# Even tables loaded to column 196 and mirrored on ScalarE; the first spread of feature D/2 made by products with a row-picking matrix

## The chip, the cores and the metric

The kernel runs on one core of a Trainium2 chip. The metric is device time in microseconds (us) of one execution, the median of several; lower is better. The engines are called as in the profile: PE is TensorE (PEld its weight loads), DVE is VectorE, ACT is ScalarE, POOL is GpSimd, SP is SyncE, which only issues transfers. They run on their own instruction streams, each in order, and wait for one another by semaphores. Transfers are issued on the queues of SP, ACT and POOL and are moved by 16 shared DMA engines.

## The reference

A Fourier mixing block over (batch 8, sequence 3136, model dimension 256), of which the real part is kept, and then a gated convolution block:

```python
X = np.fft.fft(x, axis=1)
X = np.fft.fft(X, axis=2)
x = X.real.astype(np.float32)

h = np.maximum(x @ w_in, 0.0)                       # 256 -> 1024
for k in range(3):                                  # taps along the sequence, zero padded
    conv_out += conv_w[k][None, None, :] * hp[:, k:k + S, :]
gate = 1.0 / (1.0 + np.exp(-conv_out))
return (h * gate @ w_out).astype(np.float32)        # 1024 -> 256
```

Input and output are float32, the weights come as float64 and are narrowed on the chip.

## The kernel before

**What is computed, and in which form.** Along the sequence only half of the frequencies are needed, since the input is real: per batch two tables of 128 rows by NK = 1569 columns are made, called P and Q (`PQ[b]`, tiles pt and qt). P holds 128 features of the cosine sums, Q 127 of the sine sums. The 128th row of Q's tile is not a row of Q: it holds the odd columns of the sums of feature D/2 = 128, which has no partner. The transform along the features and the matrix w_in are multiplied into one matrix G of 2 x 1024 columns (`blocks`, `column`; `ge` is the part for feature D/2). The main loop then goes through 8 batches x 4 chunks of columns x 8 blocks of 128 of the 1024 channels, 256 steps in all. In each step `seed` writes feature D/2's part, spread over all 128 partitions (`eb`), times `ge` into the accumulator pa; `products` adds two products with G into pb and pa; `copies` and `combine` form both halves of the sequence with the ReLU; `first_tap`, `middle` (a transfer that adds, issued by POOL), `last_tap`, `sigmoid` and `gate` make the gated convolution; `mm2`, five steps later, multiplies with w_out and stores.

**Where the sums along the sequence come from.** x is folded first (`fold_ops`, VectorE, `folds(0)` and `folds(1)` for the two halves of batch 0), which leaves four residues q of 98 rows each, split by even and odd frequencies. The folded data are the stationary operand; cosine and sine tables are the moving one. `tabs[0]` is the even table, 98 (or 99) partitions x 2 (cosine, sine) x 4 (q) x HE = 393 columns; `tabs[1]` the odd one with four kinds of 196 columns, of which two are loaded and two are made by ScalarE (`mirror_tables`, L305 to L310). `mend_row` halves one row of each. `scaled` (L211 to L219) makes turned copies of the folded data on ScalarE, which the `odd` units multiply with the even table at every second column. For batch 0 the units are run before the loop: four for the odd frequencies (`odd_even`, `odd`, for sine and cosine), in four parts each, so that parts 0 and 1, which need only the first half of the folds and q of 0 and 1, come ahead of parts 2 and 3; then `feature` (the even columns of feature D/2, one output row at partitions 0, 32, 64, 96), then `even_even` and `even` for sine and for cosine. Each unit has products, a copy by ScalarE and a `fin` on VectorE (on POOL for `feature`), which writes its columns of qt, pt or er.

**The spread of feature D/2.** For batch 0 its sums are put together in a one-row tile er of 1569 columns: `row` (L461) transfers the whole last row of qt there on ScalarE's queue, the `fin` of `feature` overwrites the even columns on POOL, `flip` changes signs of every fourth column on ScalarE, `store` writes er to DRAM, and `spread` loads it back, broadcast to 128 partitions, for chunks 1 to 3. Chunk 0 doesn't go through DRAM: a product of er's first 386 columns with a row of ones (`one`) spreads it, and ScalarE copies the result to `eb[0, 0]` (L941 to L945).

**Order around it.** All engines follow the order in which the program is written. At the start SP issues the loads of the first weights, of x for batch 0, then the feature matrix `dm`, the odd table (`load_odd`, four transfers), the even table (`load_even`, two transfers with whole rows of 4 x 393 columns for 48 partitions each), and then the other weights; POOL issues the few rows that are left (`rest_odd`, `rest_even`). TensorE first runs products whose result is not used (L890 to L893), until the data are there. Tiles named h come from a pool of six, tiles named g from one of seven, po from one of four accumulators.

Of the kernel before, what the change touches and what calls it, by code (L numbers as in the profile page):

```python
# [37 lines left out]
def kernel(  # L38
# [214 lines left out]
    MR = NP // 2 // 16 * 16  # L253
    assert NP == 2 * MR + 2

    def load_even(eng):

        to = tabs[0].rearrange("p s q i -> p s (q i)")
        for i in range(2):
            eng.dma_start(out=to[i:2 * MR:2], in_=dft_seq[0:MR, 0:2, HQ * i:HQ * (i + 1)]  # L260
                          .rearrange("p s q i -> p s (q i)"))

    def rest_even(eng):

# [37 lines left out]
            row = tabs[0][96:NP, st, HQ - 1] if par == 0 else tabs[1][96:NP, st, 1]  # L302
            act(row, row, AF.Copy, scale=half[96:NP])

    def mirror_tables():  # L305

        for to, of, s in ((2, 1, -1.0), (3, 0, 1.0)):
            for i in range(2):
                act(tabs[1][0:KR, to, :, i:QO:2], tabs[1][0:KR, of, :, i:QO:2], AF.Copy,
                    scale=-s if i else s)  # L310

    class Unit:

# [30 lines left out]
    def units(b):  # L344
# [83 lines left out]
        def feature():  # L428

            mms = []  # L430
            for i in range(2):
                for j, qs in enumerate(((3, 1), (2, 0))):
                    for c in range(2):
                        n = HO // 2 + 1 - c
                        o = 32 * (2 * j + c)
                        mms.append(product((slice(o, o + 1), slice(0, n)),
                                           lambda k, q, c=c: ea[b][0:k, c, q:q + 1], 0, qs[i],
                                           slice(c, HE, 2), i == 0, i == 1))

            def copy(p):  # L440
                a_["e"] = [asp.tile([P, HO + 2], F32, name="as", tag="as") for _ in range(2)]
                for j in range(2):
                    for c in range(2):
                        n = HO // 2 + 1 - c
                        o = 32 * (2 * j + c)
                        nc.scalar.copy(out=a_["e"][c][0:1, j * n:(j + 1) * n], in_=p[o:o + 1, 0:n])

            def fin(p):
                t = er[b]
                nh = HO // 2  # L450
                for c in range(2):
                    n = nh + 1 - c
                    a, bb = a_["e"][c][0:1, 0:n], a_["e"][c][0:1, n:2 * n]
                    gt(t[:, 2 * c:Q4 + 1:4], a, bb, op=ALU.add)
                    gt(t[:, M - 2 * c:Q4:-4], a[:, 0:nh], bb[:, 0:nh], op=ALU.subtract)
            return Unit(b, mms, copy, fin, True)
# [3 lines left out]

        def row():  # L461
            er[b] = erp.tile([1, NK], F32, name="er", tag="er")
            nc.scalar.dma_start(out=er[b], in_=PQ[b][1][P - 1:P, :])

        def flip():

            act(er[b][:, 3:NK:4], er[b][:, 3:NK:4], AF.Copy, scale=-1.0)

        def store():
            nc.sync.dma_start(out=ed[b:b + 1, 0:NK], in_=er[b])  # L470

        return (begin, [odd_even(1), odd(1), even_even(1), even(1), feature(), odd_even(0), odd(0),
                        even_even(0), even(0)], row, flip, store)

    class Feature:

# [201 lines left out]
            for f in self.parts(c0, c1):  # L678
                f()

    one = gp.tile([1, P], F32, name="one", tag="g")
    nc.gpsimd.memset(one, 1.0)
    ident = gp.tile([3 * NF, 3 * NF], F32, name="ident", tag="g")
    make_identity(nc, ident)
    cw24 = gp.tile([3 * NF, 1, P], F32, name="cw24", tag="g")
# [44 lines left out]
    for f in load_ops(0, 1, nc.sync, None, True):  # L730
        f()

    act(first_use, low, AF.Sigmoid)
    w_cv.narrow(0, 1)
    w_in[0].narrow(0, 2)
# [7 lines left out]
    load_even(nc.sync)  # L743
    rest_odd(nc.gpsimd)
    rest_even(nc.gpsimd)
    for i in (1, 2, 3):
        w_in[i].load(nc.sync)
    wout = const.tile([P, NF, D], F32, name="wout")
# [138 lines left out]
        gs.pop(s)  # L887


    for pool, tag, n in ((psa, "pa", 1), (psa, "pa", 1), (psb, "pb", 7)):  # L890
        p = pool.tile([P, 512], F32, name=tag, tag=tag)
        for _ in range(n):
            mm(p, w4[0][:, 0, 0:P], win[0][:, 0].rearrange("p t n -> p (t n)"), True, True)  # L893

    begin, us, row, flip, store = units(0)
    begin()

    nc.gpsimd.memset(PQ[0][1][96:P, :], 0.0)
# [11 lines left out]
    w_out = Weight(wout, moe_w_out.rearrange("(c p) o -> p c o", p=P),  # L910
                   lambda sh: xp.tile(sh, I32, name="raw", tag="xh"))
    w_out.load(nc.sync)
    blocks(0)
    column(0)
    mend_row(1, half)
    mirror_tables()
    folds(1)
    mend_row(0, half)
    for f in load_ops(1, 0, nc.sync):
        f()  # L920
    for i in range(2):
# [2 lines left out]
    for j, u in enumerate(odds):  # L924
        for i in range(2, 4):
            u.part(i)
        u.copy()
        if j == 3:
            row()
        u.fin()  # L930

    for i, u in enumerate(us[j] for j in (4, 2, 3, 7, 8)):
        u.matmuls(0, 1)
        u.copy()
        u.fin()
# [12 lines left out]
    per = len(chunks) * NF  # L948
# [197 lines left out]
```

## Time and profile before

| what | value |
|---|---|
| median of 3 runs | 1171.97 us (1171.69 to 1172.16) |
| the profiled execution's own time | 1169.8 us |
| its span | 1168.0 us |
| granted TensorE clock, mean over the span | 0.995 |
| PE busy | 1141.3 us (98%) |
| DVE busy | 975.7 us (84%) |
| ACT busy | 942.2 us (81%) |
| POOL busy | 608.9 us (52%) |
| products with w_out (po <- wout, g), 3072 instructions | 706.8 us |

The profile is of one execution; the span goes from its first instruction to its last, and all times in it count from the start of the span. A line of a timeline has the start, the duration, the engine, the line of the kernel (L93 is the helper that records every product), the operation, the tile written <- the tiles read, the shape and the number of instructions merged into it; in brackets stand the engine's idle time ahead of it and what ended it. A fp32 product is two instructions in the trace. PEclk is the share of the full TensorE clock that was granted. A wait for several semaphores is put down to the one that came last by the profile; where the engine that is named had long been done, it was another, often a transfer.

### The profile page before, as it was taken

To read this page: it belongs to the slowest core of one execution; us is meant where nothing else is said; L and a number is where in the kernel's file an instruction comes from. 1 tells how busy PE (TensorE), PEld (TensorE's weight loads), DVE (VectorE), ACT (ScalarE), POOL (GpSimd) and SP (SyncE) were. 2 spreads that over 40 slices of the span, in tenths; PEclk is the share of its full clock that TensorE was granted. 3 is DMA by queue.
4 is the path that set the end of the run, shared out by engine and by line. 5 is a ranking of instruction groups with operands and counts; after the bars stand their busy time and mean duration, and the time that the engine had idled before them with its cause. 6 is when DMAs were issued, how large, how long until landed. Compare 5 with 4: busy or idle time off the path is not lost.

```text
span 1168.0 us, 15898 instructions
## 1 busy us (share of the span) xinstructions
PE 1141.3 (98%) x4820; PEld 891.2 (76%) x4820; DVE 975.7 (84%) x1448; ACT 942.2 (81%) x1939; POOL 608.9 (52%) x738
## 2 busy tenths in 40 slices
PE   5999999999999999999999999999999999999998
PEld 3666787778778777877777777777778777777777
DVE  8699989998888889898887888779787778788885
ACT  3498878888888879888888888888887888898885
POOL 7256545676466464646455464655344344444443
PEclk9899999999999999999999999999999999999999
DMA  9667886776667686757675766856665656666654
GB/s 245 162 113 161 173 150 148 168 162 154 133 144 169 136 183 130 171 112 177 144 165 127 150 133 136 183 123 122 133 124 101 124 122 143 131 129 128 125 117 105
DMA packets 106200, 168.15 MB, mean 144 GB/s; under 512 B 31275, under 2 KB 61241, under 8 KB 106115
## 3 DMA queue, kind: packets, MB, share of 16 engines
q0 software_dynamic: 42160, 115.87, 51.6%
q1 hardware_dynamic: 63208, 51.13, 15.7%
q8 instruction: 38, 0.62, 0.2%
q14 instruction: 47, 0.39, 0.1%
q10 hardware_dynamic: 747, 0.14, 0.1%
HBM read 38.40 MB, written 25.74 MB: 55 GB/s over the span
## 4 chain that ended last, share of the span: by engine, by line
PE 79%; ACT 5%; DVE 4%; issue 2%; DMA 0%; DVEq 0%; ACTq 0%
PE po L93 49%; PE pb L93 12%; PE pa L93 12%; PE pd L93 6%; DVE g L830 1%; ACT g L845 1%; ACT nb L807 1%; ACT os L878 1%; ACT pa L786 0%; ACT g L821 0%; DVE h L815 0%; DVE g L854 0%; DMA out_dram<-os 0%; DVE xh L157 0%; DVE xh L173 0%
## 5 line engine op out<-in xcount | busy, mean ns | idle before, releaser
L93 PE MATMUL po<-wout,g 128*128 128x256 f32 x3072 | 706.8, 380 | 5.2 <-DVE g L854 4.4
L93 PEld LDWEIGHTS po<-wout,g 128*128 128x128 f32 x3072 | 581.5, 190 | 149.8 <-issue 19.3
L825 POOL DMA_DIRECT2D g<-h x256 | 227.8, 890 | 466.5 <-ACT g L821 295.4
L845 ACT ACTIVATE g<-g,cw 128x385 f32<-128x385 f32 (+2 forms) x512 | 292.3, 625 | 66.1 <-DVE g L830 65.2
L853 POOL TENSOR_TENSOR g<-g,h 128x385 f32<-128x385 f32 (+1 forms) x256 | 299.3, 1169 | 45.4 <-ACT g L845 43.8
L807 ACT ACTIVATE nb<-pb 128x386 f32<-128x386 f32 (+3 forms) x512 | 227.2, 499 | 110.4 <-PE pb L93 109.7
L815 DVE CUSTOM_DVE_ANT_0 h<-pa,nb 128x386 f32<-128x386 f32 (+3 forms) x512 | 264.5, 557 | 29.1 <-POOL h L792 20.4
L830 DVE SCALAR_TENSOR_TENSOR g<-h,cw,g 128x770 f32<-128x770 f32 (+1 forms) x256 | 282.5, 1104 | 0.0
L821 ACT ACTIVATE g<-h,cw 128x770 f32<-128x770 f32 (+1 forms) x256 | 244.5, 955 | 0.0
L93 PE MATMUL pb<-qt,G 127*128 127x387 f32 (+2 forms) x512 | 215.6, 502 | 2.1 <-ACT nb L807 1.7
L93 PE MATMUL pa<-pt,G 128*128 128x387 f32 (+2 forms) x512 | 213.2, 497 | 0.5 <-ACT pa L786 0.5
L854 DVE TENSOR_TENSOR g<-g,h 128x385 f32<-128x385 f32 (+1 forms) x256 | 190.2, 743 | 24.6 <-ACT g L845 24.5
L786 ACT ACTIVATE pa<-eb,ge 128x387 f32<-128x387 f32 (+2 forms) x256 | 155.5, 608 | 1.5 <-DVE h L815 1.2
L93 PEld LDWEIGHTS pa<-pt,G 128*128 128x128 f32 x512 | 97.4, 191 | 75.0 <-issue 18.3
L132 POOL DMA_INDIRECT xh<-in_x_dram,idx x64 | 93.8, 1466 | 20.1 <-issue 11.3
L93 PEld LDWEIGHTS pb<-qt,G 127*128 127x128 f32 x512 | 91.3, 191 | 11.0 <-ACT nb L807 4.5
L93 PE MATMUL pd<-tab,w 98*128 98x197 f32 (+2 forms) x448 | 97.8, 318 | 0.2 <-DVE as L419 0.2
L93 PEld LDWEIGHTS pd<-tab,w 98*128 98x128 f32 (+1 forms) x448 | 82.0, 191 | 9.3 <-ACT pa L786 0.6
L878 ACT COPY os<-po 128x256 f32<-128x256 f32 x196 | 57.3, 394 | 6.6 <-PE po L93 6.6
L168 DVE TENSOR_TENSOR xh<-xh 98x1024 f32<-98x1024 f32 (+1 forms) x32 | 47.9, 1497 | 0.1
L157 DVE TENSOR_TENSOR xh<-xh 98x1020 f32<-98x1020 f32 (+1 forms) x32 | 46.9, 1469 | 0.4 <-DMA xh<-in_x_dram,idx 0.4
L392 DVE TENSOR_TENSOR as<-as,pd 128x196 f32<-128x196 f32 x14 | 5.0, 359 | 36.1 <-ACT as L388 36.1
(143 smaller groups left out, 456.9 us busy)
## 6 DMA issues: line engine op xcount, KB each, us to landing
g<-h POOLq DMA_DIRECT2D x192, 385.0 KB, 4.0
g<-h POOLq DMA_DIRECT2D x64, 416.0 KB, 4.2
out_dram<-os SPq DMA_DIRECT2D x96, 256.0 KB
xh<-in_x_dram SPq DMA_DIRECT2D x16, 784.0 KB
eb<-ed SPq DMA_DIRECT2D x16, 193.5 KB
raw<-in_moe_w_in_dram SPq DMA_DIRECT2D x4, 512.0 KB
raw<-in_moe_w_out_dram SPq DMA_DIRECT2D x1, 2048.0 KB
eb<-ed SPq DMA_DIRECT2D x8, 209.0 KB
```

Of the source, the lines that this page charges most:

```text
L93: nc.tensor.matmul(o, l, r, start=start, stop=stop, skip_group_check=True)
L132: nc.gpsimd.indirect_dma_start(out=xh[b, h][0:NP, 7 - m].rearrange("p q d -> p (q d)"), out_offset=None, in_=bass.AP(tensor=x.tensor, offs ...
L786: act(pa[s][:, 0:n], eb[b, c], AF.Copy, scale=ge[:, f:f + 1])
L807: act(nb[s][:, i, cols], p[:, cols], AF.Copy, scale=-1.0 if i else 1.0)
L815: nc.vector._custom_dve(TENSOR_ADD_SAT, out=to, in0=a[:, cols], in1=c[:, i, cols], s0=BIG, s1=0.0)
L821: act(gs[s], hs[s][:, 0:n], AF.Copy, scale=cw[:, 0, s[2]:s[2] + 1])
L825: nc.gpsimd.dma_start(out=gs[s], in_=hs[s][:, 1:1 + n], accum_op=ALU.add)
L830: stt(out=g, in0=h[:, k:k + n], scalar=cw[:, k, f:f + 1], in1=g, op0=ALU.mult, op1=ALU.add)
L845: act(gs[s][:, c], gs[s][:, c], AF.Sigmoid, scale=cw[:, 1, s[2]:s[2] + 1])
L853: gt(g[:, p], g[:, p], h[:, p], op=ALU.mult)
L854: vt(g[:, v], g[:, v], h[:, v], op=ALU.mult)
L878: nc.scalar.copy(out=osb[:, j % 2], in_=pt[:, j % 2])
```

## The change

1. **Even table.** `load_even` loads only columns 0 to 196 (HM = 197 columns) of each q, in four transfers instead of two. A new function, `mirror_even(q)`, makes columns 197 to 392 on ScalarE, as a reversed copy with a sign, two instructions for each q. The rows that POOL loads (`rest_even`) come whole, as before.
2. **Odd mirrors.** `mirror_tables` takes a half h; each call makes four copies of half the size. The first call comes ahead of `blocks(0)`, the second behind `mirror_even(0)`.
3. **Filler products.** `keep_on(n)` is the old loop body with the unused products; `keep_on(2)` is run once more behind `column(0)`.
4. **First spread.** A matrix `sel` of 128 x 384 takes the place of `one`: its first 128 columns are one in row 127 and zero elsewhere, the next 128 are their negative, and of the last 128 only row 0 is used, which is one. `odd_first` multiplies it with the odd columns of qt (two products over 128 rows), `even_first` the one-row sums of `feature` with the row of ones (four products), all into one po accumulator; ScalarE copies it to `eb[0, 0]` behind `even_even(1)`.
5. **Q's row.** `row` only allocates er. `flip`, now behind all units, transfers the odd columns of Q's last row to er on SP's queue and changes signs on POOL; `store` and `spread` follow it.
6. **Smaller moves.** The memset of qt's rows 96 to 127 goes from POOL (L898) to VectorE, ahead of its first instruction; the sums of `feature` lie in a tile of the pool h instead of two of the pool as.

```diff
+    HM = HO // 2 + 1
+
     def load_even(eng):
-        to = tabs[0].rearrange("p s q i -> p s (q i)")
-        for i in range(2):
-            eng.dma_start(out=to[i:2 * MR:2], in_=dft_seq[0:MR, 0:2, HQ * i:HQ * (i + 1)]
-                          .rearrange("p s q i -> p s (q i)"))
+        for s in range(2):
+            for i in range(2):
+                eng.dma_start(out=tabs[0][i:2 * MR:2, s, :, 0:HM], in_=bass.AP(
+                    tensor=dft_seq.tensor, offset=dft_seq.offset + (s * NQ + HQ * i) * HE,
+                    ap=[[4 * NQ * HE, MR], [HE, HQ], [1, HM]]))
+
+    def mirror_even(q):
+        for st, s in enumerate(((1.0, 1.0), (-1.0, 1.0), (-1.0, -1.0), (1.0, -1.0))[q]):
+            of = st if q % 2 else 1 - st
+            act(tabs[0][0:KR, st, q, HM:HE][:, ::-1], tabs[0][0:KR, of, q, 0:HE - HM], AF.Copy, scale=s)
...
-    def mirror_tables():
+    def mirror_tables(h):
+        k = KR if h else NP
         for to, of, s in ((2, 1, -1.0), (3, 0, 1.0)):
             for i in range(2):
-                act(tabs[1][0:KR, to, :, i:QO:2], tabs[1][0:KR, of, :, i:QO:2], AF.Copy,
-                    scale=-s if i else s)
+                act(tabs[1][0:k, to, h, i:QO:2], tabs[1][0:k, of, h, i:QO:2], AF.Copy, scale=-s if i else s)
...
         def row():
             er[b] = erp.tile([1, NK], F32, name="er", tag="er")
-            nc.scalar.dma_start(out=er[b], in_=PQ[b][1][P - 1:P, :])
+
+        def odd_first(p, n):
+            for i in range(2):
+                mm(p[:, 1 + 2 * i:n:4], sel[:, i * P:(i + 1) * P], PQ[b][1][:, 1 + 2 * i:n:4], i == 0, True)
+
+        def even_first(p, n):
+            for c in range(2):
+                m = (n - 2 * c + 3) // 4
+                o = HO // 2 + 1 - c
+                for i in range(2):
+                    mm(p[:, 2 * c:n:4], sel[0:1, 2 * P:3 * P], a_["e"][c][0:1, i * o:i * o + m], False, i == 1)
 
         def flip():
-            act(er[b][:, 3:NK:4], er[b][:, 3:NK:4], AF.Copy, scale=-1.0)
+            nc.sync.dma_start(out=er[b][:, 1:NK:2], in_=PQ[b][1][P - 1:P, 1:NK:2])
+            nc.gpsimd.tensor_scalar(out=er[b][:, 3:NK:4], in0=er[b][:, 3:NK:4], scalar1=-1.0, scalar2=None, op0=ALU.mult)
...
-    one = gp.tile([1, P], F32, name="one", tag="g")
-    nc.gpsimd.memset(one, 1.0)
+    sel = gp.tile([P, 3 * P], F32, name="sel", tag="g")
...
+    begin, us, row, flip, store, odd_first, even_first = units(0)
+    begin()
+    nc.vector.memset(PQ[0][1][96:P, :], 0.0)
...
     rest_even(nc.gpsimd)
+    nc.gpsimd.iota(sel[:, 0:P], pattern=[[0, P]], base=1 - P, channel_multiplier=1,
+                   allow_small_or_imprecise_dtypes=True)
+    nc.gpsimd.tensor_scalar(out=sel[:, 0:P], in0=sel[:, 0:P], scalar1=0.0, scalar2=1.0, op0=ALU.is_equal, op1=ALU.mult)
+    nc.gpsimd.tensor_scalar(out=sel[:, P:2 * P], in0=sel[:, 0:P], scalar1=-1.0, scalar2=None, op0=ALU.mult)
+    nc.gpsimd.memset(sel[0:1, 2 * P:3 * P], 1.0)
...
+    def keep_on(n):
+        for _ in range(n):
+            mm(bank, w4[0][:, 0, 0:P], win[0][:, 0].rearrange("p t n -> p (t n)"), True, True)
+
...
-    nc.gpsimd.memset(PQ[0][1][96:P, :], 0.0)
...
+    mirror_tables(0)
     blocks(0)
     column(0)
+    keep_on(2)
     mend_row(1, half)
-    mirror_tables()
+    mirror_even(0)
+    mirror_tables(1)
     folds(1)
+    mirror_even(2)
     mend_row(0, half)
+    mirror_even(1)
+    mirror_even(3)
...
         u.copy()
-        if j == 3:
-            row()
         u.fin()
 
+    row()
+    n = chunks[0].k1
     for i, u in enumerate(us[j] for j in (4, 2, 3, 7, 8)):
         u.matmuls(0, 1)
+        if i == 0:
+            p = spare()
+            odd_first(p, n)
+        elif i == 1:
+            even_first(p, n)
         u.copy()
+        if i == 1:
+            eb[0, 0] = ebp.tile([P, HN], F32, name="eb", tag="eb")[:, 0:n]
+            nc.scalar.copy(out=eb[0, 0], in_=p[:, 0:n])
         u.fin()
-        if i == 2:
-            flip()
-            store()
-            spread(0, range(1, len(chunks)))
-
-    n = chunks[0].k1
-    p = psd.tile([P, 512], F32, name="pd", tag="pd")
-    mm(p[:, 0:n], one, er[0][:, 0:n], True, True)
-    eb[0, 0] = ebp.tile([P, HN], F32, name="eb", tag="eb")[:, 0:n]
-    nc.scalar.copy(out=eb[0, 0], in_=p[:, 0:n])
+    flip()
+    store()
+    spread(0, range(1, len(chunks)))
```

More of the change, by code (lines that the diff above doesn't have):

```diff
@@ L440, in copy @@
             def copy(p):
-                a_["e"] = [asp.tile([P, HO + 2], F32, name="as", tag="as") for _ in range(2)]
+                e = hp.tile([P, HW], F32, name="h", tag="h")
+                a_["e"] = [e[:, i * (HO + 2):(i + 1) * (HO + 2)] for i in range(2)]
                 for j in range(2):
@@ L472, in units @@
         return (begin, [odd_even(1), odd(1), even_even(1), even(1), feature(), odd_even(0), odd(0),
-                        even_even(0), even(0)], row, flip, store)
+                        even_even(0), even(0)], row, flip, store, odd_first, even_first)
     class Feature:
@@ L887, in mm2 @@
         gs.pop(s)
+    def keep_on(n):
+        for _ in range(n):
+            mm(bank, w4[0][:, 0, 0:P], win[0][:, 0].rearrange("p t n -> p (t n)"), True, True)
     for pool, tag, n in ((psa, "pa", 1), (psa, "pa", 1), (psb, "pb", 7)):
[L891 to L898, printed above, removed]
+        bank = pool.tile([P, 512], F32, name=tag, tag=tag)
+        keep_on(n)
     odds = [us[j] for j in (0, 1, 5, 6)]
```

## The prediction

> **What bounds the kernel now.** I read the page's 40 slices first (29 us each, busy tenths), then the table of stretches for idle time of TensorE and its clock. From the second slice on TensorE is full and sets the pace, and the change touches nothing there, so the question is by how much that part starts earlier.
>
> ```profile
> span 1168.0 us, 15898 instructions
> ...
> PE   5999999999999999999999999999999999999998
> ...
> 24.00:26.00 2.00, 0.00 (x0) 0.00 (x0) 1.97 (x3) 2.00 (x7) 0.52 (x1) 1.00 0.94 217
> 26.00:28.00 2.00, 1.24 (x4) 1.27 (x5) 1.97 (x4) 1.82 (x4) 1.01 (x2) 0.72 1.04 379
> 28.00:30.00 2.00, 2.00 (x7) 2.00 (x7) 0.24 (x1) 0.00 (x0) 1.16 (x2) 0.50 1.06 388
> ...
> 44.00:48.00 4.00, 4.00 (x6) 1.12 (x5) 2.80 (x6) 2.69 (x6) 0.33 (x3) 0.50 0.18 51
> ...
> 60.00:70.00 10.00, 9.08 (x39) 6.66 (x40) 9.93 (x15) 10.00 (x22) 5.53 (x8) 1.00 0.71 131
> ```
>
> After the stretch and its length come the busy times of PE, PEld, DVE, ACT and POOL, then the granted clock, the DMA share and GB/s. From 60 on three engines are nearly full. Before that TensorE has a hole at 22 to 27, and it is fed slowly at 44 to 48; the clock there is 0.50. Its timeline gives the places:
>
> ```profile
> 12.97 6.30 PE L93 MATMUL pb<-win 128*128 128x512 f32 x14
> 21.15 0.95 PE L93 MATMUL po<-dm,win 128*128 128x1 f32 x8
> 21.96 0.58 PE L93 MATMUL po<-tab,w 98*128 98x196 f32 x2
> 26.76 1.53 PE L93 MATMUL po<-tab,h 98*128 98x197 f32 x4 [4.22 <-ACT h L218]
> ...
> 32.23 0.83 PE L93 MATMUL po<-tab,w 99*128 99x196 f32 x4
> 32.90 1.57 PE L93 MATMUL po<-tab,h 98*128 98x197 f32 x8
> 34.31 0.83 PE L93 MATMUL po<-tab,w 99*128 99x196 f32 x4
> ...
> 37.27 4.85 PE L93 MATMUL po<-tab,w 99*128 99x99 f32 x32
> 43.75 1.49 PE L93 MATMUL pd<-er,one 1*128 1x386 f32 x2 [1.63 <-POOL er L454]
> ...
> 48.34 1.65 PE L93 MATMUL pb<-qt,G 127*128 127x386 f32 x2 [0.22 <-ACT nb L807]
> ...
> 51.74 1.97 PE L93 MATMUL po<-win,dm 128*128 128x256 f32 x8
> ...
> 66.38 0.92 PE L93 MATMUL pb<-qt,G 127*128 127x386 f32 x2 [0.92 <-ACT nb L807]
> ...
> 67.78 2.75 PE L93 MATMUL po<-wout,g 128*128 128x256 f32 x12
> ```
>
> The first hole is laid to ScalarE's L218, but its instructions for the first half of the folds, the only ones these products read, are over by 22.5 (below). The other operand is the even table. DMA moves it until about 26: there the rate steps from 217 to 379 GB/s, which I read as the end of the table and the next load.
>
> ```profile
> 20.75 1.71 ACT L218 ACTIVATE h<-w,turn 98x256 f32<-98x256 f32 x4 [10.16 <-POOL w L200]
> 22.37 0.62 ACT L759 COPY G<-po 128x256 f32<-128x256 f32 x2
> 22.88 0.16 ACT L769 COPY ge<-po 128x2 f32<-128x2 f32 x1
> 23.07 0.80 ACT L303 ACTIVATE tab<-tab,half 2x196 f32<-2x196 f32 x2
> 23.90 1.20 ACT L309 ACTIVATE tab<-tab 99x196 f32<-99x196 f32 x4
> 25.00 1.69 ACT L218 ACTIVATE h<-w,turn 98x256 f32<-98x256 f32 x4
> ...
> 46.83 0.71 ACT L633 ACTIVATE win<-win,low 128x512 int32<-128x512 int32 x1
> ...
> 54.54 0.93 ACT L821 ACTIVATE g<-h,cw 128x770 f32<-128x770 f32 x1
> ```
>
> At the second hole the timelines of VectorE and the list of waits show everybody waiting for one transfer, Q's row into er:
>
> ```profile
> 42.10 0.57 DVE L374 TENSOR_TENSOR qt<-as,po 128x393 f32<-128x393 f32 x1 [2.16 <-DMA er<-qt]
> ...
> 44.44 0.56 DVE L376 TENSOR_TENSOR pt<-as,po 128x392 f32<-128x392 f32 x1
> 44.91 0.42 DVE L631 TENSOR_SCALAR win<-raw 128x512 int32<-128x512 int32 x1
> ...
> 47.57 0.69 DVE L639 SCALAR_TENSOR_TENSOR win<-raw,win 128x512 int32<-128x512 int32 x1 [1.17 <-ACT win L633]
> ...
> 49.23 1.02 DVE L815 CUSTOM_DVE_ANT_0 h<-pa,nb 128x385 f32<-128x385 f32 x2
> ```
>
> **The change, part by part.** *Table.* A row of 393 columns becomes 197, so 589.5 KB x 2 x 196/393 = 588 KB (0.60 MB) less is moved before the first product of `odd`. The price per byte, and the issue:
>
> ```profile
> q1 hardware_dynamic: 168, 0.93, 104.1%
> ```
>
> ```profile
> 17.50 1.23 SPq L260 DMA_DIRECT2D tab<-dft_seq_dram  x2
> ```
>
> The first line is SP's queue in 20 to 24 us (packets, MB, share of 16 engines), the second the issue of the table. The queue moved 0.93 MB in 4 us; 0.60 MB are 2.6 us, so the table is there at about 26.7 - 2.6 = 24.1. The shorter pieces (788 bytes) could cost more; bounds 0 and 2.6 us of gain. SP issues four transfers, not two, 0.6 us each, over at 20; what waits behind them (the weight loads) is first needed at 44.91.
>
> *ScalarE.* Eight mirrors have the form of L309, 0.30 each, two per q. `mirror_tables` becomes eight of half size; between 0.16 (L769) and 0.30, I take 0.20, 0.8 per half. The order: L218 to 22.4, half of the odd mirrors to 23.2, G and ge to 24.0, `mend_row` to 24.8, mirror of q 0 to 25.3. That, not the table, then frees the product of 26.76: **1.4 us earlier**. Behind it the second half of the odd mirrors (26.1), L218 (27.8), and mirror of q 2 (28.4) are all ahead of their products.
>
> *TensorE.* `keep_on(2)` is four instructions of 6.30/14 = 0.45, from 22.1 to 23.9, then the odd product to 24.5: the hole shrinks from 4.22 to 0.8 us, and I expect full clock behind it. From 26.76 to 32.23 stand 16 instructions of `odd` and 6 of `odd_even`; at full clock they take 16 x 1.41/8 + 6 x 0.67/4 = 3.8 us (distances of the starts 32.23, 32.90, 34.31) for 5.47: **1.6 us**. So far 3.0.
>
> Added are 4 + 8 instructions of 97 columns, at 4.85/32 = 0.15 each 1.8 us (bounds 1.2 to 2.3, by the 386-column row product at half clock: 0.75/4 each). The last `even` product ends at 42.12 - 3.0 + 1.8 = 40.9. The 1.49 us at 43.75 go.
>
> *The row.* L374 no longer stands until 42.10. The last step into pt takes 1.04 us behind its product (43.96 to 45.00 before), so pt is ready at 42.0 for 45.0: **3.0 us earlier**. The seeds' spread is copied at about 37, so nothing else holds pa. VectorE from there to `combine` of step 0 took 4.32 us, 1.17 of them waiting for L633, which stood on ScalarE behind that copy and the seeds; without it 3.15: 45.1 for 49.23, **4.1 earlier**.
>
> *Step 0 to the loop.* L633 can now follow VectorE's L631 at 42.4; pb of step 1 came 1.5 us after it starts (46.83 to 48.34), so at 43.9. At full clock pb and pa take 1.4 (66.38 to 67.78), column 1 takes 0.8 (21.15 to 21.96) and blocks 1 take 2.0, to 48.1. `first_tap` of step 0 came 0.8 behind them (53.71 to 54.54): 48.9, 5.6 earlier. `combine` of step 2 waited for POOL, which waits for that tap:
>
> ```profile
> POOL g L825 <- ACT g L821: 16.1, 4, 11.4
> DVE h L815 <- POOL h L792: 2.0, 1, 2.0
> ```
>
> So the loop starts between 4.1 and 5.6 us earlier, and by the full engines of 60 to 70 nothing later wins or loses it. I take the middle, 4.8. The profiled execution has 1168.0 of span and 1.8 around it (1169.8), 2.2 under the median of 1171.97; a shift goes from each alike: **1171.97 - 4.8 = 1167.2**.
>
> *What costs nothing.* The memset of qt goes to VectorE, before its first instruction at 2.90, which waits for a transfer; 1.45 us on POOL, no more than that if uncovered. POOL gets four instructions for `sel` in its place:
>
> ```profile
> 17.58 1.45 POOL L898 MEMSET qt<- 32x1569 f32 x1
> ...
> 19.55 1.17 POOL L200 TENSOR_TENSOR w<-xh,sg 98x4 f32<-98x4 f32 x1
> ```
>
> Their price lies between nothing and 3.8 us (an iota like L898, two products like L200, a short memset). L200 reads four elements a partition and takes as long as a large VectorE instruction; I take 1.5 for the four, between the ends, and leave L200 where it is; one such slot either way moves L218 of 20.75, and all behind it, by 1.2 us. The moved transfer (`flip`) waits for qt (about 39); behind it on SP stand the store, three spreads and the loads of ft, first used with chunk 1 at step 8, behind its sign on POOL the two-element memset for step 0's h. With 2 to 3 us of travel the sign is done by 42.5, ahead of `combine` at 45.1.
>
> A rule speaks to the clock. The Trainium skill, page "TensorE: Matmul & The Clock Gate", section "Why this matters for your kernels", allows idle gaps up to about 3 us between bursts. The trace disagrees: 1.63 us before 43.75, then 0.50. By the rule the start stays warm and the gain stands at 4.8 or more; by the row two gaps near 42 (some 1.6 us together) may yet cost the clock.
>
> **Rivals.** *The clock falls again at 41 to 44.* For it: the row at 43.75. Then the 4.2 us of pb, pa, column and blocks run at half clock, for one stretch like that of 26.76 to 30 (3.4 us, 1.7 lost) or one like that of 44 to 51 (7 us, 3.5 lost). With the middle, 2.6, `first_tap` gains 3.0: 1169.0.
>
> *ScalarE, not the table, holds the first hole.* L218's second half ends at 26.69, just ahead of 26.76, as the trace's releaser says. Then the change puts 2 x 0.6 + 0.4 us of mirrors ahead of it, the product starts at 27.6 to 28.4, TensorE is idle for 3 us and cold again: 0.8 to 1.6 later instead of 3.0 earlier. The row's 3 us remain, less 1.8 of products: gain near 0.4, 1171.6. Against it: that code reads only first-half tiles.
>
> *The element-wise row blocks POOL, slower.* The new transfer is 784 separate words. Price per word from the gathers of 52 to 58 us:
>
> ```profile
> q1 hardware_dynamic: 9277, 0.04, 85.5%
> ```
>
> 0.855 x 16 x 6 us / 9277 = 8.8 ns of one engine; over 16 engines 0.4 us, on a single one 6.9, and with both sides by the word, 13.9. It decides once it lands later than some 9 us after its issue at 39: then POOL's memset, and `combine` of step 0 with it, come after 49.23. At 13.9 us and 2 of travel it lands at 55, and `combine` starts near 55.9: 6.7 later, 1178.7. Against it: three gathers of 3136 words each were through in those 6 us.
> The Trainium skill, "DMA: Bandwidth & Descriptors", "Rules for kernel authors", says that a strided last dimension lowers to one descriptor per element; the 9277 packets agree, and it speaks for this rival's count.
>
> **How the numbers follow.** Forecast, gain 3.3 to 6: 0.62, its own range 1166.0 to 1168.7. More than 6 (POOL's slot won as well): 0.07, 1165.3. Clock falls, or L200 slips a slot: 0.14, 1169.0. ScalarE holds the hole: 0.09, 1171.6. Row blocks POOL: 0.08, 1178.7. A measurement of this kernel tells 0.2% (2.3 us) from nothing, so faster means under 1169.6: 0.62 + 0.07 + 0.11 of the clock case = 0.80; the rest of it and ScalarE's case are the same, 0.12; slower 0.08. For 8 in 10 the range goes from 1165.2 to 1171.2.
>
> **What would show it.** Right: the first `odd` product near 25.3 released by the mirror of q 0, clock 1.0 from 26 to 30, L374 without a wait on er, pt at 42, `combine` at 45. Wrong: a hole of 3 us or more before the `odd` products, 0.50 after 44, SP or POOL waiting over 5 us for er, or L218 starting at 22 instead of 20.75. A first mm2 at 63 (67.78 before) with an end less than 3 us earlier would say that the loop gave the gain back.

## The result, and the profile after

| | before | after |
|---|---|---|
| median of 11 runs each, us | 1171.67 | 1167.58 |
| lowest and highest run | 1168.31 to 1172.66 | 1164.78 to 1168.27 |
| profiled execution: own time, span | 1169.8, 1168.0 | 1167.47, 1165.7 |
| a second profiled execution | 1168.31, 1166.5 | 1164.84, 1163.1 |

The ratio of the times is 0.9967, with a 95% interval from 0.9955 to 0.998; the forecast stands for 1167.2 / 1171.97 = 0.9959.

The runs after the change lie in two groups, and the mean granted clock sorts them: four at 1164.8 to 1165.1 with 0.999 or 1.000, seven at 1167.5 to 1168.3 with 0.996 or 0.997. The profiled execution is one of the seven. Its timeline of TensorE:

```profile
25.23 0.96 PE L93 MATMUL po<-tab,h 98*128 98x197 f32 x4 [0.55 <-ACT tab L270]
...
35.89 1.46 PE L93 MATMUL po<-h,sel 1*128 1x97 f32 x8
37.28 6.14 PE L93 MATMUL po<-tab,w 98*128 98x197 f32 x24
...
64.97 2.75 PE L93 MATMUL po<-wout,g 128*128 128x256 f32 x12
```

The first hole is 0.55 us instead of 4.22, and what ends it is ScalarE at L270, the helper through which the mirrors run. But the 24 products of the last even unit take 6.14 us. The table of stretches says why (the columns are those of the prediction's first fence: busy times of PE, PEld, DVE, ACT and POOL, then the granted clock):

```profile
26.00:30.00 4.00, 4.00 (x26) 4.00 (x25) 2.78 (x5) 3.95 (x12) 1.57 (x3) 1.00 1.04 397
...
34.00:38.00 4.00, 3.90 (x32) 3.39 (x25) 2.26 (x7) 2.06 (x6) 2.19 (x4) 1.00 1.00 230
38.00:40.00 2.00, 2.00 (x12) 2.00 (x11) 0.86 (x2) 0.00 (x0) 0.64 (x2) 0.66 1.01 158
40.00:44.00 4.00, 4.00 (x14) 3.56 (x13) 1.34 (x5) 1.31 (x3) 1.08 (x1) 0.50 0.18 25
44.00:48.00 4.00, 3.09 (x8) 1.49 (x7) 3.93 (x9) 1.57 (x4) 0.87 (x3) 0.81 0.05 19
```

From 26 to 30 the clock is full, as forecast. It falls inside 38 to 40, where TensorE is busy for all of the 2.00 us; in the 4.00 us ahead of that it stood for only 0.10. (A clock of 0.50 is called cold here, and the clock is said to fall when it goes there.) If the cold clock is 0.50, the cold time is the length times (1 - clock) / 0.5: 1.36 + 4.00 + 1.52 = 6.9 us, from 40 - 1.36 = 38.6 on.

The same places on ScalarE and VectorE, one fence each:

```profile
20.23 1.71 ACT L218 ACTIVATE h<-w,turn 98x256 f32<-98x256 f32 x4 [9.35 <-POOL w L200]
...
24.80 0.62 ACT L270 ACTIVATE tab<-tab 99x196 f32<-99x196 f32 x2
...
35.42 1.32 ACT L456 COPY h<-pd 1x197 f32<-1x197 f32 x4 [1.50 <-PE pd L93]
...
51.73 0.93 ACT L851 ACTIVATE g<-h,cw 128x770 f32<-128x770 f32 x1
```

```profile
39.14 0.57 DVE L383 TENSOR_TENSOR qt<-as,po 128x393 f32<-128x393 f32 x1 [1.39 <-PE po L93]
...
43.95 0.56 DVE L385 TENSOR_TENSOR pt<-as,po 128x392 f32<-128x392 f32 x1
...
47.80 1.01 DVE L845 CUSTOM_DVE_ANT_0 h<-pa,nb 128x385 f32<-128x385 f32 x2
```

The first of the two mirrors of q 0, which are started at 24.80 and are over at 25.4, frees the product of 25.23; L218 starts at 20.23. The step that was L374 is now L383, and it waits for a product, no longer for the transfer into er. From there on all is later than forecast: pt is ready at 44.5 (42.0 forecast), `combine` at 47.80 (45.1), `first_tap` at 51.73 (48.9). POOL, and the transfer of `flip` on SP's queue:

```profile
17.14 0.25 POOL L771 IOTA sel<- 128x128 f32 x1
...
19.20 0.19 POOL L775 MEMSET sel<- 1x128 f32 x1
19.56 0.64 POOL L200 TENSOR_TENSOR w<-xh,sg 98x4 f32<-98x4 f32 x1
...
42.92 1.94 POOL L490 TENSOR_SCALAR er<-er 1x392 f32<-1x392 f32 x1 [4.28 <-DMA er<-qt]
44.73 0.14 POOL L822 MEMSET h<- 128x2 f32 x2
```

```profile
33.54 0.60 SPq L489 DMA_DIRECT2D er<-qt  x1
```

The four instructions for `sel` take 2.25 us from first to last (1.5 assumed), and L200 isn't put off by them. The element-wise transfer is issued as soon as the odd columns stand, at 33.5 and not at 39, and POOL gets its data at 42.9: 9.4 us, where 2 to 3 were assumed. POOL's memset at 44.73 is still 3 us ahead of `combine`, which needs it.

A second profile of the same kernel belongs to the other group. Its clock at 38 to 40, then its TensorE, VectorE and ScalarE:

```profile
38.00:40.00 2.00, 2.00 (x16) 2.00 (x15) 1.29 (x3) 0.60 (x2) 0.00 (x0) 1.00 1.00 121
```

```profile
35.77 1.13 PE L93 MATMUL po<-h,sel 1*128 1x97 f32 x8
36.83 3.96 PE L93 MATMUL po<-tab,w 98*128 98x197 f32 x24
...
62.23 2.75 PE L93 MATMUL po<-wout,g 128*128 128x256 f32 x12
```

```profile
41.31 0.56 DVE L385 TENSOR_TENSOR pt<-as,po 128x392 f32<-128x392 f32 x1
...
45.48 1.01 DVE L845 CUSTOM_DVE_ANT_0 h<-pa,nb 128x385 f32<-128x385 f32 x2
```

```profile
34.17 1.32 ACT L456 COPY h<-pd 1x197 f32<-1x197 f32 x4 [0.43 <-PE pd L93]
...
36.27 0.32 ACT L367 COPY as<-po 128x197 f32<-128x197 f32 x1 [0.78 <-ACT h L456]
...
48.99 0.93 ACT L851 ACTIVATE g<-h,cw 128x770 f32<-128x770 f32 x1
```

Here the same 24 products take 3.96 us and everything behind them keeps the forecast's hours: pt 41.9, `combine` 45.5, `first_tap` 49.0, first mm2 62.2 (63). The two executions are 2.74 us apart at the first mm2 and 2.6 at the end. The largest difference ahead of the fall is at the one-row copies of `feature` (L456). In the first profile, where the clock falls, ScalarE pauses ahead of them and they come at 35.42; in the second it pauses behind them and they come at 34.17. The eight one-row products read those copies. In the first profile they run from 35.89 to the next start at 37.28 (1.39 us): a weight load among them waits 0.3 us for the last copies, and TensorE stands for the 0.10 us named above. In the second they run from 35.77 to 36.83 (1.06 us) without a gap. The clock falls at 38.6, some 1.3 us after the last of them.

### The profile page after: what moved, and what is told of

It is laid out like the page before. It is cut to its first block, busy times and chain, and to the rows that moved or that the text cites. A ratio compares the mean times of both kernels' runs of the same rounds, so it can differ in the third digit from the quotient of the medians.

```text
span 1165.7 us, 15936 instructions
## 1 busy us (share of the span) xinstructions
PE 1143.1 (98%) x4834; PEld 892.4 (77%) x4834; DVE 978.5 (84%) x1449; ACT 943.7 (81%) x1950; POOL 604.7 (52%) x741
## 4 chain that ended last, share of the span: by engine, by line
PE 79%; ACT 5%; DVE 4%; issue 2%; DVEq 0%; ACTq 0%
PE po L93 50%; PE pb L93 12%; PE pa L93 12%; PE pd L93 6%; DVE g L860 1%; ACT g L875 1%; ACT nb L837 1%; ACT os L908 1%; ACT pa L816 0%; DVE h L845 0%; ACT g L851 0%; DVE g L884 0%; DVE xh L168 0%; DVE w L194 0%; DVE xh L157 0%
## 5 line engine op out<-in xcount | busy, mean ns | idle before, releaser
L883 POOL TENSOR_TENSOR g<-g,h 128x385 f32<-128x385 f32 (+1 forms) x256 | 294.5, 1151 | 44.5 <-ACT g L875 42.8
L132 POOL DMA_INDIRECT xh<-in_x_dram,idx x64 | 91.0, 1421 | 20.1 <-issue 11.4
L194 DVE TENSOR_TENSOR w<-xh 98x508 f32<-98x508 f32 (+1 forms) x32 | 35.1, 1097 | 0.1
```

Source lines behind the costliest of these rows:

```text
L132: nc.gpsimd.indirect_dma_start(out=xh[b, h][0:NP, 7 - m].rearrange("p q d -> p (q d)"), out_offset=None, in_=bass.AP(tensor=x.tensor, offs ...
L883: gt(g[:, p], g[:, p], h[:, p], op=ALU.mult)
```

## The experiments

**The question** was what lowers the clock at 38.6, and by its mean in seven runs of eleven. First theory: the eight products of `even_first` use one row of the array of 128 and count for little in whatever sets the clock, so that the stretch about 36 counts as idle although TensorE is busy. Rival: the short stop of ScalarE, with the gaps that it makes. The second question was what each part of the change is worth.

**Second looks.** The kernel after, unchanged:

> The changed kernel as it is, for a second profile. If the fall of the clock hangs on where the gauge's windows lie, it shows either a clock of 1.0 throughout, even products of 3.6 to 4.0 us and a time of 1165.0, or the fall again near the one-row products and 1168.0; nothing between.

It gave 1164.84 us and the second set of rows above. The kernel before, unchanged:

> The kernel before as it is, for a second profile. The one at hand (1169.8) has two cold stretches, 26.9 to 30.3 and 44.0 to 50.8. Runs of 1171.7 to 1172.7 should have more of them (clock 0.992): a third stretch, or longer ones; a run near 1168.5 fewer.

It gave 1168.31 us, with these stretches (the columns as above):

```profile
24.00:28.00 4.00, 1.48 (x5) 1.51 (x6) 3.93 (x6) 3.91 (x10) 1.53 (x4) 0.54 1.00 299
28.00:32.00 4.00, 4.00 (x16) 4.00 (x15) 0.34 (x1) 0.00 (x0) 2.56 (x4) 0.60 1.06 389
...
44.00:48.00 4.00, 3.84 (x6) 1.32 (x6) 3.22 (x7) 2.87 (x6) 0.67 (x4) 0.60 0.12 38
48.00:52.00 4.00, 3.84 (x20) 3.11 (x20) 3.90 (x9) 2.03 (x6) 0.00 (x0) 0.97 0.51 164
```

By the same working the first hole cost 3.68 + 3.20 = 6.9 us of cold clock here and the second 3.20 + 0.24 = 3.4. The cold stretches come in pieces of about 3.4 us: one, or two. Fewer cold stretches were expected of a run this fast, and that is a miss: the first profile of this kernel has three pieces too, one behind the first hole and two behind the second, and took 1.5 us longer. So it matters where a piece lies. Here the first one begins at 28 - 3.68 = 24.3, and TensorE stands until 26.52 in any case, so 2.2 us of cold clock cost nothing: by half speed 1.1 of the 1.5 us, an estimate from these rows. The Trainium skill, page "TensorE: Matmul & The Clock Gate", section "What's actually happening", speaks of a free-running window of about 3.4 us by which activity is watched; the stretches agree. One piece lowers the mean clock of a run by 3.44 x 0.5 / 1168 = 0.0015. So this run (0.996) has three pieces as counted, a run after with 0.9965 has two, and a run of before with 0.992 would have about five; wherever the clock of a run of before from 1171.6 us up is on record, it is 0.992 (0.993 once), but none of these runs was profiled.

**The one-row products over all 128 rows.** The sums of `feature` lie in an h tile that is set to zero first, and the last 128 columns of `sel` are zero except in row 0. The same sums are computed.

```diff
         def row():
             er[b] = erp.tile([1, NK], F32, name="er", tag="er")
+            e = hp.tile([P, HW], F32, name="h", tag="h")
+            nc.vector.memset(e[:, 0:2 * (HO + 2)], 0.0)
+            a_["e"] = [e[:, i * (HO + 2):(i + 1) * (HO + 2)] for i in range(2)]
...
-                    mm(p[:, 2 * c:n:4], sel[0:1, 2 * P:3 * P], a_["e"][c][0:1, i * o:i * o + m], False, i == 1)
+                    mm(p[:, 2 * c:n:4], sel[:, 2 * P:3 * P], a_["e"][c][:, i * o:i * o + m], False, i == 1)
...
+    nc.vector.memset(sel[:, 2 * P:3 * P], 0.0)
```

> The changed kernel's clock fell to 0.5 from 38.7 to 45.5 us although TensorE was busy. Theory A: the clock's gauge counts how much of the array works, and the one-row products (h,sel, 1.46 us) starve it. Here the same products run over 128 rows, of which 127 are zero, with the same count and length: the clock stays at 1.0, the 24 even products take 3.6 us instead of 6.14, and every run is near 1165.0. Rival B (the gauge counts streamed columns against weight loads, whatever the rows): the fall stays, two groups of runs at 1165 and 1168. Rival C (the value or the phase of the run alone decides): the same as B.

Measured: 1164.64 us (1164.11 to 1165.06, 6 runs), ratio 0.995 (0.9935 to 0.9965); mean clock 0.999 or 1.000 in every run. TensorE's timeline:

```profile
35.68 1.05 PE L93 MATMUL po<-h,sel 128*128 128x97 f32 x8
36.57 3.89 PE L93 MATMUL po<-tab,w 98*128 98x197 f32 x24
```

Eight products over 128 rows take no longer than eight over one (1.05 against 1.13), and in no run did the clock fall. Both rivals named in the expectation had the fall stay. But two memsets and the place of `row()` were changed with the products, which the next run takes apart.

**The same, with the products over one row again**: only the changed `mm` line is put back.

```diff
-                    mm(p[:, 2 * c:n:4], sel[:, 2 * P:3 * P], a_["e"][c][:, i * o:i * o + m], False, i == 1)
+                    mm(p[:, 2 * c:n:4], sel[0:1, 2 * P:3 * P], a_["e"][c][0:1, i * o:i * o + m], False, i == 1)
```

> The twin of e1_full_rows: everything as there, its two memsets too, but the products of the even part read one row again. Theory A (few rows at work starve the clock's gauge): runs at 1165 and at 1168 again, over a third of them slow. Rival (the memsets of e1_full_rows or the order that they make moved something, not the rows): every run near 1164.6, as there.

Measured: five runs at 1164.82 to 1165.21 with 0.999 or 1.000, three at 1167.87 to 1168.12 with 0.996 (median 1165.1, ratio 0.9957, 0.9944 to 0.997). The second group is back, and with it the 3 us. So the memsets do not keep the clock, and between this kernel and the one above only the rows are left. The pair by itself (3 of 8 against 0 of 6) could still be chance. Counted over all kernels that have the same steps up to here, but for those memsets in the kernel after: the clock fell in 10 of 20 runs with one row (7 of 12 after, 3 of 8 here) and in 0 of 18 over all rows (the kernel above and the last two below). What these runs leave open is the part of the late copies: every profile taken over all rows has the copies early, so none shows whether full rows also hold the clock when the copies come late.

**A filler ahead of the one-row products**: two instructions of full size.

```diff
         elif i == 1:
+            keep_on(1)
             even_first(p, n)
```

> One unused product of 512 columns over the whole array is put ahead of the one-row products; it costs 0.9 us at full clock. Theories A and B: the gauge is fed, the clock stays, every run near 1165.0 + 0.9 = 1165.9. Rival C: the fall stays in about as many runs as before, groups at 1165.9 and 1168.9.

Measured: ten of twelve runs at 1165.70 to 1166.33, with 0.999 or 1.000, two at 1169.4 and 1169.6 with 0.997; median 1166.03, ratio 0.9967 (0.9955 to 0.9978). Most falls are gone, for about 1 us of filler; two remained. The filler seems to make the fall rarer (2 of 12 runs against 7 of 12), though so few runs don't settle it; filled rows made it absent in these runs.

**The table part alone** (with filler and split mirrors): Q's row is transferred on ScalarE's queue and spread by the product with `one`, as before.

```diff
+            nc.scalar.dma_start(out=er[b], in_=PQ[b][1][P - 1:P, :])
...
-            nc.sync.dma_start(out=er[b][:, 1:NK:2], in_=PQ[b][1][P - 1:P, 1:NK:2])
-            nc.gpsimd.tensor_scalar(out=er[b][:, 3:NK:4], in0=er[b][:, 3:NK:4], scalar1=-1.0, scalar2=None, op0=ALU.mult)
+            act(er[b][:, 3:NK:4], er[b][:, 3:NK:4], AF.Copy, scale=-1.0)
...
+    mm(p[:, 0:n], one, er[0][:, 0:n], True, True)
```

> The table part alone (short even table, mirrors, filler), with the old transfer of Q's row and the product with the row of ones. My sum: the odd products end 3.0 us earlier as in the changed kernel, the row's transfer is issued at 33.6; if it travels 5.3 us as before, L374's like starts at 39 and the time is near 1169. Rival: the transfer lands when the loads ahead are through, near 41, and the gain is 1 us: 1171.

Measured: 1167.59 us (1165.87 to 1169.48, 12 runs), ratio 0.9975 (0.9964 to 0.9985); better than expected. The issue on ScalarE's queue, the wait on VectorE and the product of the row on TensorE:

```profile
32.52 0.76 ACTq L473 DMA_DIRECT2D er<-qt  x1
```

```profile
39.39 0.56 DVE L383 TENSOR_TENSOR qt<-as,po 128x393 f32<-128x393 f32 x1 [3.74 <-DMA er<-qt]
...
41.64 0.56 DVE L385 TENSOR_TENSOR pt<-as,po 128x392 f32<-128x392 f32 x1
```

```profile
41.04 1.65 PE L93 MATMUL pd<-er,one 1*128 1x386 f32 x2 [3.06 <-POOL er L464]
```

The row lands at about 39.3 instead of 42.0, 6.8 us after its issue, and pt is ready at 42.2. With the shorter table the odd products and the row come earlier together, and the wait for the row ends pt 0.3 us later than the twelve products that take its place. What it does leave is the hole of 3.06 us and cold clock behind it: the product of the row takes 1.65 us here, against 0.91 where the clock holds, as it does in the kernel before with fillers, below.

**The spread part alone** (with filler): the table is loaded whole and no even mirrors are made.

```diff
-        for s in range(2):
-            for i in range(2):
-                eng.dma_start(out=tabs[0][i:2 * MR:2, s, :, 0:HM], in_=bass.AP(
...
+        to = tabs[0].rearrange("p s q i -> p s (q i)")
+        for i in range(2):
+            eng.dma_start(out=to[i:2 * MR:2], in_=dft_seq[0:MR, 0:2, HQ * i:HQ * (i + 1)]
+                          .rearrange("p s q i -> p s (q i)"))
...
-    mirror_even(0)
...
-    mirror_even(2)
...
-    mirror_even(1)
-    mirror_even(3)
```

> The new spread alone (with the filler and the split odd mirrors), the even table loaded whole. My sum: the first product of odd stays at 26.7, released by the table; behind it the clock stays at 1.0 thanks to the filler, so the even products end at 42.1 - 1.6 + 1.8 = 42.3 and pt is ready at 43.4 for 45.0: 1169 to 1170 if the clock holds later, 1171 to 1172 if it falls. Rival (ScalarE, not the table, held that product): it comes at 25 to 25.5 here too and the time equals the changed kernel's.

Measured: 1167.82 us (1165.86 to 1170.13, 12 runs), ratio 0.9977 (0.9964 to 0.9989).

```profile
26.77 0.94 PE L93 MATMUL po<-tab,h 98*128 98x197 f32 x4 [2.40 <-DMA tab<-dft_seq_dram]
```

```profile
26.00:30.00 4.00, 3.23 (x19) 3.26 (x20) 2.35 (x4) 2.33 (x5) 2.03 (x3) 1.00 1.05 380
```

With the filler in the hole and the table as before, TensorE is freed by the table's transfer, at the hour of before (26.76). This row decides the forecast's second rival: ScalarE did not hold the first hole, for its second set of L218 goes on until 27.2 here, behind the product's start. The profile is of one of the fastest runs, and in it a gap of 2.40 us is followed by full clock. Four runs of the twelve lie at 1167.3 to 1167.9, three of them with 0.998, and five at 1168.9 to 1170.1 with 0.995 to 0.997, so in other runs the clock did fall.

**The same, over all rows**: the table loaded whole again, on top of the full-row kernel, so that, as far as the runs above go, only the first hole is left to cost clock.

```diff
-                eng.dma_start(out=tabs[0][i:2 * MR:2, s, :, 0:HM], in_=bass.AP(
...
+            eng.dma_start(out=to[i:2 * MR:2], in_=dft_seq[0:MR, 0:2, HQ * i:HQ * (i + 1)]
...
-    mirror_even(0)
```

> e1_full_rows with the even table loaded whole and no even mirrors: what the table part is worth where the clock holds later. The first product of odd comes at 26.7 instead of 25.1, released by the table: 1.6 us, 1166.2, and more where the longer gap ahead of it costs the clock. Rival (the delay is hidden behind a later wait): 1164.6 to 1165.

Measured: 1167.27 us (6 runs), ratio 0.9964 (0.995 to 0.9977): five at 1166.96 to 1167.51, one at 1165.36. TensorE's row and the stretches of a run of the five:

```profile
26.74 0.93 PE L93 MATMUL po<-tab,h 98*128 98x197 f32 x4 [2.07 <-DMA tab<-dft_seq_dram]
```

```profile
26.00:30.00 4.00, 3.26 (x15) 3.29 (x16) 3.29 (x5) 2.55 (x6) 1.80 (x3) 0.80 1.06 385
30.00:34.00 4.00, 4.00 (x20) 4.00 (x19) 0.56 (x2) 0.32 (x1) 3.09 (x4) 0.77 1.05 387
```

A gap of 2.07 us is followed by one cold piece (1.60 + 1.84 = 3.4 us). The table part is worth 2.6 us at the median of this pair (1167.27 to 1164.64), but the one run at 1165.36, with 0.999, is only 0.7 us over it: as far as one run tells, most of the 2.6 goes through the clock.

**No filler**: the full-row kernel without `keep_on(2)`.

```diff
     column(0)
-    keep_on(2)
     mend_row(1, half)
```

> e1_full_rows without the two filler products behind the first column. TensorE then stands about 2.8 us ahead of the odd products instead of 1.0. If such a gap costs the clock as the gap of 4.22 did, 3.4 us run at half speed behind it and 1.6 us are lost: 1166.2, in all or most runs. Rival (the gap is too short for the gauge): 1164.6.

Measured: 1166.89 us (1166.19 to 1167.43, 6 runs), ratio 0.9963 (0.995 to 0.9976): three runs at 1166.2 to 1166.6 with 0.998, three at 1167.2 to 1167.4 with 0.996 or 0.997. The profile is of the slowest.

```profile
25.31 1.68 PE L93 MATMUL po<-tab,h 98*128 98x197 f32 x4 [2.71 <-ACT tab L270]
```

```profile
24.00:26.00 2.00, 0.69 (x2) 0.69 (x3) 1.97 (x4) 1.96 (x10) 0.81 (x2) 0.54 0.90 261
26.00:30.00 4.00, 4.00 (x14) 4.00 (x13) 3.22 (x5) 3.95 (x12) 1.88 (x3) 0.50 1.03 394
30.00:34.00 4.00, 4.00 (x22) 4.00 (x22) 0.63 (x2) 0.99 (x4) 3.09 (x4) 0.88 1.07 349
```

The hole is 2.71 us, and here two cold pieces lie in it and behind it (1.84 + 4.00 + 0.96 = 6.8 us). By their clock the three faster runs had one piece, and they lie near the 1166.2 that was expected for one. The four unused instructions are worth 1166.89 - 1164.64 = 2.2 us, by themselves nearly as much as the table. The Trainium skill, page "TensorE: Matmul & The Clock Gate", section "Why this matters for your kernels", allows gaps of up to about 3 us, as the prediction said; this gap is inside that, and the clock fell in all six runs.

**The kernel before, with fillers in both holes.**

```diff
     column(0)
+    keep_on(4)
...
+    keep_on(2)
     n = chunks[0].k1
     p = psd.tile([P, 512], F32, name="pd", tag="pd")
     mm(p[:, 0:n], one, er[0][:, 0:n], True, True)
```

> The kernel before with unused full-size products in its two holes (four behind the first column, two ahead of the product with the row of ones) and nothing else: what the clock alone is worth. Theory: most of the gain of either part of the change is the clock. Then the odd products (still released by the table near 26.7) run at full clock, 1.6 us less, the row still lands near 42, and the products behind it run at full clock, some 2 us less up to the first tap: near 1168, for a median of 1170 to 1172 before. Rival (the transfers that the change removes make the gain, the clock little): 1170 or more.

Measured: 1171.12 us (12 runs), ratio 0.9995 (0.9982 to 1.0009): five runs at 1167.49 to 1168.12 with 0.999 or 1.000, seven at 1171.04 to 1171.9 with 0.995. The profile is of the first group, with a clock of 1.00 all through from 24 to 52; TensorE and VectorE:

```profile
43.40 0.91 PE L93 MATMUL pd<-er,one 1*128 1x386 f32 x2 [1.23 <-POOL er L454]
```

```profile
41.75 0.57 DVE L374 TENSOR_TENSOR qt<-as,po 128x393 f32<-128x393 f32 x1 [3.48 <-DMA er<-qt]
```

So where the clock held, the kernel before takes 1167.7, and the change's order of work is worth 1167.7 - 1165.0 = 2.7 us. But fillers alone did not hold the clock in seven of twelve runs, and the median hardly moved: a miss. Behind which of the holes the clock fell in those seven was not seen. The row's landing did not move either (41.75 for 42.10), though here the last products of the odd units start 1.6 us earlier (35.60 for 37.27 at the 32 products behind them). That speaks for the loads ahead of it, which the table part makes shorter, as what sets its hour; no run moves those loads alone.

**Two steps further.** In the full-row kernel POOL's change of sign lies beside VectorE's narrowing of a weight. The sign was moved to ScalarE, behind the copies of step 0, with the store and the loads behind it.

```diff
-            nc.gpsimd.tensor_scalar(out=er[b][:, 3:NK:4], in0=er[b][:, 3:NK:4], scalar1=-1.0, scalar2=None, op0=ALU.mult)
+
+        def sign():
+            act(er[b][:, 3:NK:4], er[b][:, 3:NK:4], AF.Copy, scale=-1.0)
...
-    store()
-    spread(0, range(1, len(chunks)))
...
+    sign()
+    store()
+    spread(0, range(1, len(chunks)))
```

> e1_full_rows with the sign of er's odd columns on ScalarE behind the copies of step 0 instead of on POOL. There POOL's instruction took 2.11 us (43.22 to 45.33), and two VectorE instructions beside it 1.25 and 0.88 us where 0.69 and 0.42 are usual. If POOL slows VectorE, these 1.0 us come back: 1163.6. Rival (VectorE was slow for another reason, or its delay is taken up at the next wait for POOL): 1164.6.

Measured: 1164.44 us (1164.29 to 1164.69, 6 runs), ratio 0.9943 (0.993 to 0.9955); 0.2 us better than the full-row kernel, where 1.0 was expected: a miss, and the rival's case. VectorE in the full-row kernel, then in this one:

```profile
43.56 1.25 DVE L678 SCALAR_TENSOR_TENSOR win<-raw,win 128x512 f32<-128x512 f32 x1
44.74 0.88 DVE L655 TENSOR_SCALAR win<-raw 128x512 int32<-128x512 int32 x1
```

```profile
43.93 0.69 DVE L680 SCALAR_TENSOR_TENSOR win<-raw,win 128x512 f32<-128x512 f32 x1
44.54 0.42 DVE L657 TENSOR_SCALAR win<-raw 128x512 int32<-128x512 int32 x1
...
51.22 1.02 DVE L849 CUSTOM_DVE_ANT_0 h<-pa,nb 128x385 f32<-128x385 f32 x2 [0.58 <-POOL h L826]
```

Both instructions take about half as long when POOL doesn't work beside them, 1.0 us less in all. VectorE then stands for 0.58 us at the third `combine`, waiting for POOL's h, which waits for `first_tap`. The slack was VectorE's, not the chain's.

Last, on top of it, the narrowing of the second block of w_in was put behind the products and copies of step 0, so that TensorE's step 1 is not held by ScalarE:

```diff
-    for f in w_in[1].parts(0, 2, room):
-        f()
...
+    for f in w_in[1].parts(0, 2, room):
+        f()
     sign()
```

> e7_sign_on_act with step 0's products and copies ahead of the narrowing of the second weight block. There the copies of nb stood on ScalarE behind an instruction that waits for VectorE, and TensorE waited 1.34 us for them ahead of step 1. If TensorE's way to blocks 1 and the first tap now sets the start, pb of step 1 comes 1.3 us earlier, column 1 then waits for the narrowed weights (44.6), and the tap comes 0.5 us earlier: 1163.9. Rival (VectorE sets it): 1164.4 or a little later, since VectorE's narrowing is not moved.

Measured: 1163.97 us (1163.86 to 1164.11, 6 runs), ratio 0.9947 (0.9931 to 0.9964), with 0.999 or 1.000 in all.

```profile
42.13 0.92 PE L93 MATMUL pb<-qt,G 127*128 127x386 f32 x2
```

The pb of step 1 comes at 42.13 with no wait (43.80, after a wait of 1.34, in the kernel above), and the time is the 1163.9 that was expected. This run and the one above were on different chips, so the 0.5 us between them has that doubt. It is the fastest kernel of the study, 3.6 us under the median of the change as made (2.9 of them by the rows alone).

## Why the prediction was right, and where it was not

The median is 1167.58 for a forecast of 1167.2, inside the narrow range, and the direction was right. Step by step:

- **Table.** Right. The first `odd` product came at 25.23 (25.3), freed by the mirror of q 0; the shorter pieces cost nothing that shows.
- **Filler and clock from 26 to 30.** Right: the hole was 0.55 us, the clock 1.00. In the full-row kernel without the filler they were 2.71 and 0.50.
- **Twelve products for the spread.** Right in time: the last `even` product ends at 40.8 (36.83 + 3.96) in the second profile, 40.9 forecast.
- **The row.** Right as a wait, wrong as a gain of its own. L383 waits no more for er, and pt came at 41.9 where the clock held (42.0). But the table part alone had pt at 42.2 (its last step started at 41.64), so of the 3.0 us which the forecast laid to the row 2.8 would have come without it: the parts share one gain. The lowest time of each kernel says the same: 1167.5 before with fillers, 1165.9 with either part, 1164.8 with both, so 1.6 + 1.6 came to 2.7.
- **From pt to the loop.** Right where the clock held: `combine` 3.75 us earlier (4.1), `first_tap` 5.55 (5.6). The middle of the two, 4.8, was taken; the spans of that profile and of the first one before differ by 1168.0 - 1163.1 = 4.9.
- **The step that failed: "a shift goes from each alike"**, with the clock full behind 26. The sum 1169.8 - 4.8 = 1165.0 is where four runs of eleven lie; the other seven have two cold pieces, some 2.9 us, that the sum does not hold. On the other side most runs of before lie at 1171.6 to 1172.7, where the clock on record is 0.992 in all runs but one, more cold time than the profile from which the sum was made (0.995). The two about cancel between the medians: 4.1 us against 4.8. That the median came out 0.4 us from the forecast is luck to that extent.
- **The first rival** (the clock falls again, 1169.0) is thus what most runs did, but not by its mechanism: not by gaps near 42, but some 3 us earlier, with TensorE busy, and the runs show that the one-row products are part of it. Why it falls only in about half of the runs stays open. ScalarE's pause ahead of the copies goes with it in the two profiles; what makes ScalarE pause there was not found.
- **The second rival** is refuted by the spread part alone: the table, not ScalarE, held the hole. The kernel after says so too: its first `odd` product starts at 25.23, ahead of the second set of L218 (26.07).
- **The third rival** was closer than its chance: the words took 9.4 us from issue to use, about the 9 from which it decides, where 2 to 3 were assumed. No row stood behind that 2 to 3; Q's row in the kernel before took 5.4 (issued at 36.74, used at 42.10). It was the hour that saved the forecast here. SP waits only for the odd columns, so the transfer is issued at 33.5 and not at 39, and POOL's wait of 4.28 us (4.98 in the second profile) ends ahead of what anybody needs.

## What to carry to other kernels

A time that moves by 3 us from run to run on an unchanged kernel can be a clock that falls in some runs; sort the runs by their granted clock before subtracting medians, and forecast from a profile whose clock is known. A product that picks one row can as well run over all rows: here zeros in the other 127 cost nothing that shows, and the clock never fell in 18 runs. Fillers of full size made falls rarer in some places and did not stop them in others. Where two parts shorten the same stretch, cost them together: each alone gave 1.6 of the 2.7 us of both.

## What was unexpected of the hardware

- The clock fell with TensorE busy for all but 0.10 us of the 4.6 us ahead: with eight products over one row it fell in 10 of 20 runs, with the same eight over 128 rows, of which 127 are zero, in 0 of 18.
- Cold stretches lasted 3.4 or 6.8 us. Gaps of 2.07 and 2.71 us were enough for them, but not always: one run of the kernel with the former nearly escaped (1165.36), and in the profile of the spread part alone the clock stayed full behind a gap of 2.40.
- A transfer of 784 words took 9.4 us from issue to use beside other loads (DMA share 1.01 until 40), a contiguous row of 1569 words 6.8.
- POOL's change of sign over 392 elements of one row took 1.9 to 2.1 us beside a busy VectorE (ScalarE did the same in 0.92), and two VectorE instructions beside it took 1.25 and 0.88 us instead of 0.69 and 0.42.
